# A squared-ReLU layer as seven block products: the second layer of blocks 1 to 8 with fewer multiplications and more sums

## The chip, the cores and the metric

The kernel runs on one NeuronCore of a Trainium2 chip. A core has a matrix engine (TensorE, in the profile PE, with its weight loads shown as PEld), three engines for elementwise work (VectorE or DVE, ScalarE or ACT, GpSimd or POOL) and a queue engine (SyncE or SP) that issues most transfers. Each engine works through its own instructions in order and waits for others by semaphores. PE writes into PSUM, eight banks of 128 partitions x 512 fp32 values; DVE and ACT read PSUM, POOL does not. The metric is the time of one execution in microseconds of device time. Before the change its median is 312.25 us in three runs (311.99 to 312.39).

## The reference

Attention over a sliding window of 64 positions (8 batches, 8 heads, 576 positions, head size 64), and on its output a feed-forward layer with a squared ReLU. All inputs and the output are fp32.

```python
scores = scale * np.matmul(q, k.transpose(0, 1, 3, 2))
mask = (rel >= 0) & (rel < window)          # window = 64
attn = softmax(np.where(mask, scores, -1e9))
x = np.matmul(attn, v).transpose(0, 2, 1, 3).reshape(4608, 512)
h = np.maximum(x @ w_in, 0.0)               # w_in  512 x 2048
out = (h * h) @ w_out                       # w_out 2048 x 512
```

## The kernel before

The 4608 tokens are nine blocks of 512: blocks 0 to 7 are the first 512 positions of each batch, and block 8 collects the last 64 of all batches. A block has four attention units (pairs of heads, `hp`), then layer 1 and layer 2. Everything that PE multiplies is fp16, and it sums in fp32.

Small functions each do one step of one unit or block, and the kernel calls them in an order written out by hand, which is each engine's order of work:

- `T` transposes q and k of a unit on PE (blocks 1 and 2; later blocks are transposed by DMA), and ACT or DVE copies them out of PSUM (`qk`).
- `Sc` multiplies q and k into `at_ps[i]`, two tiles of two banks, and ACT takes the exponential (`pm`, L281). `M` applies the mask as a minimum (DVE, L288). `AV` multiplies with v, again into `at_ps[i]`, and `N` divides (DVE, L311 and L314, `xs`); `A` is both. `X` transposes `xs` on PE into the bank of `ps_tr` and ACT or DVE copies it into `xT`.
- `F1(g, f)` is chunk f of layer 1: four matmuls of 512 columns into one of the two `ps_f1` banks (L337); DVE takes the positive part (`hr`, L340), ACT squares it into `h2` (L341). A block has 16 chunks.
- `F2(g, ts, quarter, ...)` is a quarter of layer 2 for 128 tokens: four matmuls of 512 columns (L372). After the fourth quarter ACT scales the bank into `osb` (L376) and SP stores it. A block has 16 such calls. `F2_last` does the last 128 tokens in two halves of 256 columns (L388), to store the first earlier.

Block 0 runs alone at first. Then F2 of block 0 runs beside the attention of block 1, F1 of block 1 beside that of block 2, written out call by call. From there a loop over n = 1 to 8 takes F2 of block n and F1 of block n + 1 together. The string `order` says which comes when ("2" an F2 call, "1" an F1 call); the list `fill` made from it has 32 entries, called slots here. `put(i, ...)` hangs other work in front of slot i: Sc, M, A and X of block n + 2, two units at a time. So Sc of two units stands at slot 8, M at 11 and 12, A of both at 14, X at 18 and 20, and the other two units ten slots later.

Inputs arrive as fp32 in staging tiles of 128 x 512 (`piece`, 24 of them), are cast to fp16 (mostly by POOL) and, for q and k of blocks 3 to 8, transposed by a DMA. `next_part` issues one load, its cast, and the transpose of the piece four before; a rule in the loop sets how many are issued by each slot. Loads, transposes and stores all stand in SP's queue, in program order. A tile pool gives a buffer again only when everything that reads it is done.

Of the kernel before, what the change touches and what calls it, by code (L numbers as in the profile page):

```python
# [8 lines left out]
FP32 = mybir.dt.float32  # L9
# [6 lines left out]
def kernel(  # L16
# [23 lines left out]
    X_SCALE = 16.0  # L40
# [4 lines left out]
    stp = ctx.enter_context(tc.tile_pool(name="stp", bufs=24))  # L45
    p16p = ctx.enter_context(tc.tile_pool(name="p16p", bufs=8))
# [270 lines left out]
    def X(g, hp, engine=nc.scalar, pool=ps_tr, tag="tr"):  # L317
# [3 lines left out]
        tr = pool.tile([P, 2, 512], FP16, name="xtr", tag=tag)  # L321
# [46 lines left out]
    def F2(g, ts, quarter, pool, tag):  # L368
# [5 lines left out]
        if quarter == 3:  # L374
            osb = opool.tile([P, DM], FP32, name="osb", tag="osb", bufs=5)
            nc.scalar.activation(out=osb[:], in_=f2[g, ts][:], func=AF.Copy, scale=OUT_SCALE)  # L376
            to_store.append((g, ts, osb))
        if quarter == 1 or g == seq[-1]:
            while to_store:
                store(*to_store.pop(0))  # L380

    def F2_last(g, ts):

        for half, (pool, tag) in enumerate(((ps_f2, "f2"), (ps_f1, "f1"))):
            cols = slice(half * 256, half * 256 + 256)
            t = pool.tile([P, 512], FP32, name="ops", tag=tag)
            for f in range(FFC):
                nc.tensor.matmul(t[:, 0:256], h2[g][:, f, ts * P:(ts + 1) * P], w_out_sb[:, f, cols],  # L388
                                 start=(f == 0), stop=(f == FFC - 1))
            osb = opool.tile([P, DM], FP32, name="osb", tag="osb", bufs=5)  # L390
            nc.scalar.activation(out=osb[:, 0:256], in_=t[:, 0:256], func=AF.Copy, scale=OUT_SCALE)  # L391
            for par, queue in enumerate((nc.sync, nc.scalar)):
                r = (2 * ts + par) * S + 512
                queue.dma_start(out=out[r:r + 64, cols], in_=osb[par * 64:(par + 1) * 64, 0:256])
# [5 lines left out]
    with tc.manual_schedule():  # L400
# [84 lines left out]
        for hp in range(2):  # L485
            cast_qk_pair(g1, "q", hp, nc.gpsimd)
            cast_qk_pair(g1, "k", hp, nc.gpsimd)
# [69 lines left out]
        F(8, second); T(g1, 2, engine=nc.vector); F(1, second)  # L557
# [13 lines left out]
        for _ in range(8):  # L571
            next_part()
        F(3, first)
# [91 lines left out]
```

## Time and profile before

| | before |
|---|---|
| time, median of three runs | 312.25 us |
| span of the profiled execution | 309.2 us |
| PE, DVE, ACT, POOL busy | 299.9, 162.7, 171.6, 117.5 us |
| layer 1 matmuls of 512 columns (L337) | 560, busy 137.6 us |
| layer 2 matmuls of 512 columns (L372) | 560, busy 136.1 us |
| layer 2 matmuls of 256 columns (L388) | 32, busy 3.7 us |
| hr (L340), squares (L341), osb (L376): mean of one | 689, 630, 587 ns |
| granted TensorE clock | 1.000 |

The profile is of one execution. The busy time of an engine counts overlapping instructions once; matmuls are pipelined, so the mean duration of one (379 ns for 512 columns) is longer than the distance from one to the next, and costs are read from distances. The span leaves out what lies before the first and after the last instruction; the profiled execution's own whole time is not given apart from its span, so the median stands beside it. The profile's chain of waits goes back from the last instruction to what released each one, and the engine that holds most of it sets the time.

### The profile page before, as it was taken

What the parts mean: (1) busy time and instruction counts of PE and PEld (TensorE: products, weight loads), DVE (VectorE), ACT (ScalarE), POOL (GpSimd) and SP (SyncE); (2) the same over time, 40 slices, a digit from 0 to 9 for tenths busy, and PEclk for the clock granted to TensorE, in tenths of its full rate; (3) what the DMA queues carried; (4) which work ended last, traced back from release to release, by engine and by line L of the source; (5) the groups of instructions that cost most, each with busy time, mean ns of one, the idle gap of its engine ahead of it and who ended that gap; (6) DMA issues with size and microseconds to landing.
All of it is one profiled execution on the core that took longest, in us unless ns stands there. A gap on an engine that the chain in (4) does not pass through costs nothing.

```text
span 309.2 us, 6624 instructions
## 1 busy us (share of the span) xinstructions
PE 299.9 (97%) x2604; PEld 150.8 (49%) x2604; DVE 162.7 (53%) x278; ACT 171.6 (55%) x268; POOL 117.5 (38%) x212
## 2 busy tenths in 40 slices
PE   7899999999999999999999999999999999999995
PEld 5444445454445544544454444544554555444444
DVE  4676628587266727553755365537553655344300
ACT  4757736686367545753575367546744674444411
POOL 4578749963462382254365246322320000000000
PEclk9999999999999999999999999999999999999999
DMA  7999999999999998999998999999921001100023
GB/s 231 241 354 375 384 289 280 310 188 175 235 182 225 178 224 187 204 194 202 197 232 187 211 187 184 205 220 173 217 58 70 34 2 36 68 34 34 36 63 74
DMA packets 141759, 55.49 MB, mean 179 GB/s; under 512 B 125728, under 2 KB 134176, under 8 KB 141728
## 3 DMA queue, kind: packets, MB, share of 16 engines
q1 hardware_dynamic: 141568, 54.94, 82.8%
q8 instruction: 20, 0.33, 0.5%
q10 hardware_dynamic: 160, 0.13, 0.2%
q14 instruction: 11, 0.09, 0.1%
HBM read 38.80 MB, written 9.44 MB: 156 GB/s over the span
## 4 chain that ended last, share of the span: by engine, by line
PE 81%; ACT 0%; DVE 0%; issue 0%
PE hps L337 36%; PE ops L372 35%; PE at L304 3%; PE at L274 3%; PE xtr L323 2%; PE ops L388 1%; PE tr L243 0%; PE hps L353 0%; PE at L337 0%; ACT osb L376 0%; DVE xT L113 0%; ACT osb L391 0%
## 5 line engine op out<-in xcount | busy, mean ns | idle before, releaser
L340 DVE TENSOR_SCALAR hr<-hps 128x512 f32<-128x512 f32 x143 | 97.9, 689 | 107.6 <-PE hps L337 106.4
L341 ACT ACTIVATE h<-hr 128x512 f16<-128x512 f32 x144 | 90.3, 630 | 86.8 <-DVE hr L340 86.6
L337 PE MATMUL hps<-xT,w_in_sb 128*128 128x512 f16 x560 | 137.6, 379 | 0.2
L372 PE MATMUL ops<-w_out_sb,h 128*128 128x512 f16 x560 | 136.1, 379 | 0.3 <-ACT osb L376 0.3
L372 PEld LDWEIGHTS <-h 128*128 128x128 f16 x560 | 53.1, 98 | 61.5 <-issue 0.3
L337 PEld LDWEIGHTS <-w_in_sb 128*128 128x128 f16 x564 | 53.1, 98 | 59.2 <-issue 1.4
L113 POOL CAST v_ev<-st_v 128x512 f16<-128x512 f32 x34 | 23.5, 692 | 43.9 <-DMA st_v<-in_v_dram 43.9
L113 POOL CAST k<-st_k 128x512 f16<-128x512 f32 x36 | 23.1, 641 | 44.7 <-DMA st_k<-in_k_dram 44.4
L281 ACT ACTIVATE pm<-at 128x1024 f16<-128x1024 f32 x35 | 34.1, 1015 | 2.7 <-PE at L274 2.7
L376 ACT ACTIVATE osb<-ops 128x512 f32<-128x512 f32 x35 | 20.5, 587 | 25.2 <-PE ops L372 25.2
L314 DVE TENSOR_TENSOR xs<-at,rden 128x512 f16<-128x512 f32 x36 | 24.9, 691 | 1.2
L288 DVE TENSOR_TENSOR pm<-pm,mask 128x1024 f16<-128x1024 f16 x32 | 24.1, 768 | 2.5 <-ACT pm L281 2.5
L111 ACT ACTIVATE xT<-xtr 128x512 f16<-128x512 f16 x31 | 18.4, 593 | 8.1 <-PE xtr L323 8.1
L113 POOL CAST q<-st_q 128x512 f16<-128x512 f32 x31 | 18.3, 609 | 10.9 <-DMA st_q<-in_q_dram 8.8
L222 POOL CAST v_od<-st_v 64x512 f16<-64x512 f32 x30 | 19.0, 635 | 1.6
L304 PEld LDWEIGHTS <-pm 128*64 128x64 f16 x576 | 11.4, 110 | 8.8 <-issue 4.3
L323 PEld LDWEIGHTS <-xs 128*128 128x128 f16 x144 | 10.7, 98 | 7.5
L304 PE MATMUL at<-v_ev,pm 128*64 128x65 f16 x384 | 14.3, 198 | 0.0
L323 PE MATMUL xtr<-ident,xs 128*128 128x128 f16 x144 | 13.8, 219 | 0.0
L113 POOL CAST v_od<-st_v 64x384 f16<-64x384 f32 x23 | 12.3, 536 | 1.8 <-DMA st_v<-in_v_dram 0.7
L304 PE MATMUL at<-v_od,pm 128*64 128x65 f16 x192 | 10.4, 194 | 0.4 <-DVE v_od L113 0.3
L111 ACT ACTIVATE qk<-tr 128x1024 f16<-128x1024 f16 x7 | 7.1, 1013 | 5.5 <-PE tr L243 3.1
(55 smaller groups left out, 120.4 us busy)
## 6 DMA issues: line engine op xcount, KB each, us to landing
st_k<-in_k_dram SPq DMA_DIRECT2D x40, 256.0 KB, 3.9
st_q<-in_q_dram SPq DMA_DIRECT2D x32, 256.0 KB, 5.1
out_dram<-osb SPq DMA_DIRECT2D x32, 256.0 KB, 2.8
st_v<-in_v_dram SPq DMA_DIRECT2D x28, 256.0 KB, 3.8
st_w<-in_moe_w_out_dram SPq DMA_DIRECT2D x16, 256.0 KB, 5.4
st_v<-in_v_dram SPq DMA_DIRECT2D x24, 128.0 KB, 4.9
w_st<-in_moe_w_in_dram SPq DMA_DIRECT2D x4, 512.0 KB, 6.1
st_w<-in_moe_w_in_dram SPq DMA_DIRECT2D x8, 256.0 KB, 7.6
```

The source lines that it names most:

```text
L111: engine.activation(out=out, in_=in_, func=AF.Copy, scale=1.0)
L113: engine.tensor_copy(out=out, in_=in_)
L281: nc.scalar.activation(out=p[:, hh, :] if apart else p[:], in_=sc[hh] if apart else both[:], func=AF.Exp, scale=1.0 / float(D) ** 0.5)
L288: nc.vector.tensor_tensor(out=p[:], in0=p[:], in1=m.unsqueeze(1).broadcast_to([P, 2, 512]), op=ALU.min)
L304: nc.tensor.matmul(a[jj * 64:(jj + 1) * 64, hh, jp * VW:jp * VW + D + 1], pm[g, hp][:, hh, j * 64:(j + 1) * 64], vsel, start=True, stop=True)
L314: nc.vector.tensor_tensor(out=x[:].rearrange("p j h d -> p h j d"), in0=a[:, :, :, 0:D], in1=rden[:].unsqueeze(3).broadcast_to([P, 2, 4, D ...
L323: nc.tensor.transpose(out=tr[:, 0, jp * P:(jp + 1) * P], in_=xs[g, hp][:, jp, :, :], identity=ident[:])
L337: nc.tensor.matmul(hps[:], w_in_sb[:, c, f * P:(f + 1) * P], xT[g][:, c, :], start=(c == 0), stop=(c == DMC - 1))
L340: nc.vector.tensor_scalar(out=hr[:], in0=hps[:], scalar1=0.0, scalar2=None, op0=ALU.max)
L341: nc.scalar.activation(out=h2[g][:, f, :], in_=hr[:], func=AF.Square)
L372: nc.tensor.matmul(f2[g, ts][:], h2[g][:, f, ts * P:(ts + 1) * P], w_out_sb[:, f, :], start=(f == 0), stop=(f == FFC - 1))
L376: nc.scalar.activation(out=osb[:], in_=f2[g, ts][:], func=AF.Copy, scale=OUT_SCALE)
```

## The change

Layer 2 of a block multiplies A (512 tokens x 2048) with B (2048 x 512). The change cuts both into 2 x 2 blocks (256 tokens, 1024 of the inner dimension, 256 columns) and computes the four blocks of the result with seven products in place of eight, after Strassen and Winograd. Four sums of blocks of B (`T_sum`, once for the whole kernel, each 128 partitions x 2048 fp16) and four sums of blocks of A (`S_sum`, for each block and each half s of 128 tokens, each 128 x 1024 fp16) are made by DVE. A product is eight matmuls of 256 columns for 128 tokens. A block has seven products for each of two halves s, in the order 1, 2, 6, 5, 7, 3, 4 (`L2S`).

Products 1, 6, 7 and 4 add up in half s of the bank `chain`; 2, 5 and 3 use the two halves of the bank `side`. After each product the bank's present sum is scaled into `osb` by ACT (products 1, 6, 5, 4) or added to what `osb` holds by DVE (2, 7, 3). Stores are issued at product 6 of each half, for the tiles finished by then. `chain` keeps the one `ps_f2` bank and `side` the one `ps_tr` bank for the rest of the kernel, so X goes into the first bank of its unit's own `at_ps` tile. `F2_last` is gone; block 0 still uses F2.

`fill` has 30 entries ("2" is now a product), and 14 in the last block. The S sums of half 0 of block n + 1 stand at slots 17 (27 in block 1) and 28, those left at slots 3 to 7 of its own layer 2. X comes at slots 16 and 17, and 27 and 28. T sum 1 stands in F2 of block 0, two calls before T of block 1's unit 2; T sums 2, 3 and 4 stand in F1 of block 1, before its chunk 0, before its chunk 7 and after its chunk 10, S3 of block 1 right behind the last of them, and S1, S2 and S4 behind chunk 15.

The sums need 32 KB per partition. The staging tiles go from 24 to 10, and the space of the sums serves as 16 more for the first 60 pieces; four casts of block 1 are called earlier for that, in the same place of POOL's order. The fp16 buffers of q and k go from 8 to 6 each. The scale of x goes from 16 to 8.

```diff
--- before.py
+++ after.py
-    X_SCALE = 16.0
+    X_SCALE = 8.0
...
-    stp = ctx.enter_context(tc.tile_pool(name="stp", bufs=24))
-    p16p = ctx.enter_context(tc.tile_pool(name="p16p", bufs=8))
+    stp = ctx.enter_context(tc.tile_pool(name="stp", bufs=10))
+    p16p = ctx.enter_context(tc.tile_pool(name="p16p", bufs=6))
...
+    wsum = const.tile([P, 8, 512], FP32, name="wsum")
+    hsum = const.tile([P, 8, 512], FP32, name="hsum")
+    T_sb = wsum[:].bitcast(FP16).rearrange("p a b -> p (a b)").rearrange("p (k c d) -> p k c d", k=4, c=8)
+    S_sb = hsum[:].bitcast(FP16).rearrange("p a b -> p (a b)").rearrange("p (k c d) -> p k c d", k=4, c=8)
+    staged = [0]
     def piece(*key):
-        st[key] = stp.tile([P, 512], FP32, name="st_" + "".join(str(x)[0] for x in key[:1]), tag="st")
+        k = staged[0] % 26
+        staged[0] += 1
+        if staged[0] > 60 or k < 10:
+            st[key] = stp.tile([P, 512], FP32, name="st_" + "".join(str(x)[0] for x in key[:1]), tag="st")
+        elif k < 18:
+            st[key] = wsum[:, k - 10, :]
+        else:
+            st[key] = hsum[:, k - 18, :]
...
-    def X(g, hp, engine=nc.scalar, pool=ps_tr, tag="tr"):
+    def X(g, hp, engine=nc.scalar, pool=ps_tr, tag="tr", own=None):
         if g not in xT:
             xT[g] = xtpool.tile([P, DMC, 512], FP16, name="xT", tag="xT")
-        tr = pool.tile([P, 2, 512], FP16, name="xtr", tag=tag)
+        if own is not None:
+            tr = at_ps[own][:, 0, :].bitcast(FP16).rearrange("p (a b) -> p a b", a=2)
+        else:
+            tr = pool.tile([P, 2, 512], FP16, name="xtr", tag=tag)
...
-            to_store.append((g, ts, osb))
-        if quarter == 1 or g == seq[-1]:
+            to_store.append(lambda: store(g, ts, osb))
+        if quarter == 1:
             while to_store:
-                store(*to_store.pop(0))
-    def F2_last(g, ts):
...
+                to_store.pop(0)()
...
+    HF = FFC // 2
+    HC = DM // 2
+    osbs = {}
+    def b_of(i, j):
+        return w_out_sb[:, i * HF:(i + 1) * HF, j * HC:(j + 1) * HC]
+    def a_of(g, i, j, s):
+        t0 = 256 * i + 128 * s
+        return h2[g][:, j * HF:(j + 1) * HF, t0:t0 + 128]
+    def t_of(k):
+        return T_sb[:, k - 1]
+    def s_of(k, s):
+        return S_sb[:, k - 1, :, 128 * s:128 * s + 128]
+    def minus(out, a, b, op=ALU.subtract, engine=None):
+        (engine or nc.vector).tensor_tensor(out=out, in0=a, in1=b, op=op)
+    def T_sum(k):
+        if k == 1:
+            minus(t_of(1), b_of(0, 1), b_of(0, 0))
+        elif k == 2:
+            minus(t_of(2), b_of(1, 1), t_of(1))
+        elif k == 3:
+            minus(t_of(3), b_of(1, 1), b_of(0, 1))
+        else:
+            minus(t_of(4), b_of(1, 0), t_of(2))
+    def S_sum(g, k, s):
+        if k == 1:
+            minus(s_of(1, s), a_of(g, 1, 0, s), a_of(g, 1, 1, s), ALU.add)
+        elif k == 2:
+            minus(s_of(2, s), s_of(1, s), a_of(g, 0, 0, s))
+        elif k == 3:
+            minus(s_of(3, s), a_of(g, 0, 0, s), a_of(g, 1, 0, s))
+        else:
+            minus(s_of(4, s), a_of(g, 0, 1, s), s_of(2, s))
+    def product(to, a, b, start):
+        for f in range(HF):
+            nc.tensor.matmul(to, a[:, f, :], b[:, f, :], start=start and f == 0, stop=f == HF - 1,
+                             skip_group_check=True)
+    def flush():
+        while to_store:
+            to_store.pop(0)()
+    def L2S(g, p, s, banks):
+        chain, side = banks
+        c, pa, pb = chain, side[:, 0:HC], side[:, HC:2 * HC]
+        lo, hi = slice(0, HC), slice(HC, 2 * HC)
+        def scaled(out, in_):
+            nc.scalar.activation(out=out, in_=in_, func=AF.Copy, scale=OUT_SCALE)
+        def plus(o, in_):
+            nc.vector.scalar_tensor_tensor(out=o, in0=in_, scalar=OUT_SCALE, in1=o, op0=ALU.mult, op1=ALU.add)
+        if p == 1:
+            for i in range(2):
+                osbs[s, i] = opool.tile([P, DM], FP32, name="osb", tag="osb", bufs=5)
+        up, dn = osbs[s, 0], osbs[s, 1]
+        if p == 1:
+            product(c, a_of(g, 0, 0, s), b_of(0, 0), True)
+            scaled(up[:, lo], c)
+        elif p == 2:
+            product(pa, a_of(g, 0, 1, s), b_of(1, 0), True)
+            plus(up[:, lo], pa)
+        elif p == 6:
+            product(c, s_of(2, s), t_of(2), False)
+            scaled(up[:, hi], c)
+            flush()
+        elif p == 5:
+            product(pb, s_of(1, s), t_of(1), True)
+            scaled(dn[:, hi], pb)
+        elif p == 7:
+            product(c, s_of(3, s), t_of(3), False)
+            plus(dn[:, hi], c)
+        elif p == 3:
+            product(pb, s_of(4, s), b_of(1, 1), False)
+            plus(up[:, hi], pb)
+            to_store.append(lambda: store(g, s, up))
+            if g == seq[-1]:
+                flush()
+        else:
+            product(c, a_of(g, 1, 1, s), t_of(4), False)
+            scaled(dn[:, lo], c)
+            if g == seq[-1] and s == 1:
+                for par, queue in enumerate((nc.sync, nc.scalar)):
+                    r = (2 * (2 + s) + par) * S + 512
+                    queue.dma_start(out=out[r:r + 64, lo], in_=dn[par * 64:(par + 1) * 64, lo])
+            else:
+                to_store.append(lambda: store(g, 2 + s, dn))
+                if g == seq[-1]:
+                    flush()
+        if g == seq[-1] and s == 1 and p == 7:
+            for par in range(2):
+                r = (2 * (2 + s) + par) * S + 512
+                nc.sync.dma_start(out=out[r:r + 64, hi], in_=dn[par * 64:(par + 1) * 64, hi])
+    ORDER = (1, 2, 6, 5, 7, 3, 4)
...
+        for hp in range(2):
+            cast_qk_pair(g1, "q", hp, nc.gpsimd)
+            cast_qk_pair(g1, "k", hp, nc.gpsimd)
...
-        F(8, second); T(g1, 2, engine=nc.vector); F(1, second)
+        F(6, second); T_sum(1); F(2, second); T(g1, 2, engine=nc.vector); F(1, second)
...
+        T_sum(2)
         F(3, first)
         Sc(g2, 0); F(1, first); T(g2, 1); F(1, first); M(g2, 0); F(2, first)
+        T_sum(3)
         Sc(g2, 1); A(g2, 0); F(1, first); T(g2, 2); F(1, first); M(g2, 1); F(2, first)
-        X(g2, 0, nc.vector)
+        X(g2, 0, nc.vector); T_sum(4)
         for _ in range(4):
             next_part()
-        Sc(g2, 2); A(g2, 1); F(1, first); T(g2, 3); F(1, first); M(g2, 2); F(2, first)
-        X(g2, 1, nc.vector); F(1, first)
+        S_sum(g1, 3, 0)
+        Sc(g2, 2); A(g2, 1); F(1, first); T(g2, 3); F(1, first); M(g2, 2); F(3, first)
+        X(g2, 1, nc.vector)
+        for k in (1, 2, 4):
+            S_sum(g1, k, 0)
...
+        chain = ps_f2.tile([P, 512], FP32, name="chain", tag="f2")
+        side = ps_tr.tile([P, 512], FP32, name="side", tag="tr")
         for n in range(1, NBLK):
             g = seq[n]
             one = seq[n + 1] if n < NBLK - 1 else None
+            second = iter([lambda p=p, s=s: L2S(g, p, s, (chain[:, s * HC:(s + 1) * HC], side))
+                           for s in range(2) for p in ORDER])
             if one is not None:
-                first = [lambda f=f: F1(one, f) for f in range(FFC)]
-                second = [lambda ts=ts, i=i: F2(g, ts, i, ps_f2, "f2") for ts in range(4) for i in range(4)]
-                a, b = iter(first), iter(second)
-                order = ("2222" + "11" + 2 * "212121211" + "21221211" if n > 1 else
-                         "22222222" + 2 * "11211211212" + "11")
-                fill = [next(a if c == "1" else b) for c in order]
+                a = iter([lambda f=f: F1(one, f) for f in range(FFC)])
+                order = ("22222222" + "11211121112111211" + "11122" if n == 1 else
+                         ("222121121211211" if n == 2 else "221212112121211") + "212121121121122")
             else:
-                fill = [lambda ts=ts, i=i: F2(g, ts, i, *((ps_f2, "f2") if ts % 3 == 0 else (ps_f1, "f1")))
-                        for ts in range(3) for i in range(4)] + [lambda: F2_last(g, 3)]
+                order = "2" * 14
+            fill = [next(a if c == "1" else second) for c in order]
             at = {}
             def put(i, *work):
@@ -605,28 +718,35 @@
             if n == 1:
                 put(0, lambda: Sc(g2, 3), lambda: A(g2, 2))
                 put(2, lambda: M(g2, 3))
-                put(3, lambda: X(g2, 2))
-                put(4, lambda: A(g2, 3))
-                put(6, lambda: X(g2, 3))
-            for work in later:
-                put(1, work)
+                put(3, lambda: X(g2, 2, own=1))
+                put(5, lambda: A(g2, 3))
+                put(7, lambda: X(g2, 3, own=1))
+            for i, work in enumerate(later):
+                put(1 + i, work)
             later = []
+            for i, (k, s) in zip((3, 4, 5, 6, 7) if n > 1 else (1, 1, 2, 4, 6),
+                                 ((4, 0), (1, 1), (2, 1), (3, 1), (4, 1))):
+                if n > 1 or (k, s) != (4, 0):
+                    put(i, lambda k=k, s=s: S_sum(g, k, s))
+            if one is not None:
+                put(27 if n == 1 else 17, lambda: S_sum(one, 3, 0))
+                put(28, lambda: S_sum(one, 1, 0), lambda: S_sum(one, 2, 0))
             base = 4 * (n + 2)
-            for i, x, two in ((12 if n == 1 else 8, (9, 11) if n == 1 else (10, 12), units[base:base + 2]),
-                              (21 if n == 1 else 18, (9, None) if n == 1 else (10, 12), units[base + 2:base + 4])):
+            for i, x, two in ((12 if n == 1 else 8, (8, 9), units[base:base + 2]),
+                              (22 if n == 1 else 19, (None, None) if n == 1 else (8, 9), units[base + 2:base + 4])):
                 for t, u in enumerate(two):
                     if u is not None:
                         put(i, lambda u=u, t=t: Sc(*u, i=t))
                         put(i + 3 + t, lambda u=u: M(*u))
                         put(i + 6, lambda u=u, t=t: A(*u, i=t))
                         if x[t] is None:
-                            later.append(lambda u=u: X(*u))
+                            later.append(lambda u=u, t=t: X(*u, own=t))
                         else:
-                            put(i + x[t], lambda u=u: X(*u))
+                            put(i + x[t], lambda u=u, t=t: X(*u, own=t))
             for i, group in enumerate(fill):
                 for work in at.pop(i, []):
                     work()
-                total = 12 + (32 * (n - 1) + i + 1) * (len(load_list) - 12) // 150
+                total = 12 + (30 * (n - 1) + i + 1) * (len(load_list) - 12) // 140
```

More of the change, by code (lines that the diff above doesn't have):

```diff
@@ L376, in F2 @@
             nc.scalar.activation(out=osb[:], in_=f2[g, ts][:], func=AF.Copy, scale=OUT_SCALE)
-            to_store.append((g, ts, osb))
-        if quarter == 1 or g == seq[-1]:
+            to_store.append(lambda: store(g, ts, osb))
+        if quarter == 1:
             while to_store:
-                store(*to_store.pop(0))
-    def F2_last(g, ts):
[L384 to L394, printed above, removed]
+                to_store.pop(0)()
```

3 lines of the change are left out of this document (removed).

## The prediction

> **What bounds the kernel now.** I read the busy shares and the chain of waits first, then the groups of instructions, then stretches of the timeline. The first three lines are the page's busy shares and the chain that ended last.
>
> ```profile
> PE 299.9 (97%) x2604; PEld 150.8 (49%) x2604; DVE 162.7 (53%) x278; ACT 171.6 (55%) x268; POOL 117.5 (38%) x212
> ...
> PE 81%; ACT 0%; DVE 0%; issue 0%
> PE hps L337 36%; PE ops L372 35%; PE at L304 3%; PE at L274 3%; PE xtr L323 2%; PE ops L388 1%; PE tr L243 0%; PE hps L353 0%; PE at L337 0%; ACT osb L376 0%; DVE xT L113 0%; ACT osb L391 0%
> ```
>
> PE is the bound, and half of it is layer 2. Next, DVE has 47% of the span free, but not evenly. Stretches of the span, with each engine's busy time: the first layer of block 1, then one whole later block.
>
> ```profile
> 56.47:74.46 17.99, 17.93 (x203) 9.48 (x203) 14.67 (x26) 15.18 (x22) 11.69 (x20) 1.00 1.08 230
> 173.41:204.75 31.34, 31.34 (x273) 15.38 (x272) 16.49 (x28) 17.68 (x28) 13.66 (x23) 1.00 1.11 199
> ```
>
> The columns are length, PE, PEld, DVE, ACT and POOL. In the early stretch DVE is free for only 3.3 us. In a later block PE is never idle and DVE is free for 14.9 us. Third, what a 256-column matmul costs, and how long a bank stays shut. The timeline at the kernel's end, then around 78 us (us of start, us of length):
>
> ```profile
> 301.61 3.59 PEld L388 LDWEIGHTS <-h 128*128 128x128 f16 x32
> 301.82 3.66 PE L388 MATMUL ops<-w_out_sb,h 128*128 128x256 f16 x32
> ...
> 303.82 0.38 ACT L391 ACTIVATE osb<-ops 128x256 f32<-128x256 f32 x1 [1.15 <-PE ops L388]
> ```
>
> ```profile
> 77.13 1.03 PE L372 MATMUL ops<-w_out_sb,h 128*128 128x512 f16 x4
> ...
> 78.20 0.60 ACT L376 ACTIVATE osb<-ops 128x512 f32<-128x512 f32 x1 [0.27 <-PE ops L372]
> ...
> 78.84 1.89 PE L372 MATMUL ops<-w_out_sb,h 128*128 128x512 f16 x8 [0.31 <-ACT osb L376]
> ```
>
> 32 loads and matmuls run in (305.2-301.8)/31 = 110 ns each (first and last start), so the 98 ns load hides behind the matmul. A 512-column one takes 216 ns (four in 0.864 us, the later blocks' step). PE finishes feeding the bank at 77.13+0.86 = 77.99; the eviction starts 0.2 later, and PE enters the same bank again only at 78.84. Last, two DVE stretches: what PE waits for at 46 us, and what the mask's minimum costs.
>
> ```profile
> 44.67 1.23 DVE L113 COPY qk<-tr 128x1024 f16<-128x1024 f16 x1 [0.46 <-PE tr L243]
> ```
>
> ```profile
> 45.95 0.41 PE L274 MATMUL at<-qk 64*128 64x64 f16 x16 [0.46 <-DVE qk L113]
> ```
>
> ```profile
> L288 DVE TENSOR_TENSOR pm<-pm,mask x32: 676/682/1101, 36.6 to 254.6; 128x1024 f16<-128x1024 f16 x32
> ```
>
> The minimum is the trace's only fp16 operation of two tensors in SBUF: 0.68 us per 1024 elements, up to 1.10.
>
> **The change part by part.**
>
> *Fewer columns.* Layer 2 of a block was 64 matmuls of 512: 64 x 0.216 = 13.82 us. It becomes 7 products x 2 halves x 8 = 112 matmuls of 256: 112 x 0.110 = 12.29 us. That is 1.54 less in seven blocks; the last one had 48 x 0.216 + 32 x 0.110 = 13.88 and saves 1.59. **-12.3 us**, all of it on PE.
>
> *DVE's new work per block.* Eight S sums of 1024 fp16 elements at 0.68 to 0.77 (median and mean of the minimum): 5.4 to 6.2. Six additions into osb: 256 fp32 columns, bounded by rden's 0.20 (8 columns) and xs' 0.69 (512 columns) and taken between them by columns, 0.44: 2.6. 16.5 becomes 24.5 to 25.3 of some 31 us. ACT loses four evictions of 0.58 and gains eight of 0.38: +0.7, no matter. So DVE fits in the mean; what counts is where its queue is late.
>
> *Neighbours on one bank.* The order 1,2,6,5,7,3,4 alternates between the chain and side banks, but 4 and the next 1 are both on chain. From the last column fed, the eviction starts 0.25 later (303.82 against 301.82+16x0.11 = 303.57), runs 0.38, and PE enters some 0.04 after: 0.67. Within the sequence a product of 0.88 lies between and hides it, if ACT or DVE comes at once. At the ends of blocks 1 to 7 nothing lies between (fill ends "22", and begins "2"), nor in the last block's middle. In blocks 2 to 6 ACT must first finish the copy of the X at slot 28, which leaves it some 0.15 late. 5 x 0.82 + 3 x 0.67 + 0.4 (block 1, an X between) = **+6.5**. The ends are 0, if only the same columns shut a bank (1 writes the other half), and 8 x 0.85 + 0.4 = 7.2 by the 512-column row. I take the wait: chain is one tile in one bank, and the nearest row is a bank waited for as a whole. The Trainium skill ("PSUM — Partial Sum Buffer", PSUM bank collisions raise a hardware error) says to guard PSUM by bank and quadrant, not by address. By that rule this term stays; guarded by address it would be 0. No run so far shows which.
>
> *X in its own bank.* ps_tr goes to side for good. X writes the bank that its unit's AV and N have left, so only the next Sc into it waits, for X's copy on ACT. At slot 19 that is near: hr, square, copy, copy stand behind two N (0.2+0.69 each), so X's second copy ends about 0.25 after PE gets there. Blocks 2 to 6: **+1.3** (0 to 2.5). Slot 8 follows X by nine slots, free.
>
> *T sum 1* (2048 elements, twice the minimum less one start: 1.25 us; 0.68 to 2.2) stands in front of the qk copy at 44.67, whose end PE already waits for. DVE comes free from the q cast at 44.22, so the copy starts at 45.4 to 45.9: **+1.0** (0 to 1.8).
>
> *T sums 2 to 4 and S3* fall into 56.47:74.46: 3 x 1.25 + 0.68 = 4.4 us against 3.3 free, so 1.1 at least if every gap is filled. They aren't: T sum 4, S3 and an N stand before the hr of chunk 11, and F1 of chunk 13 needs that bank (two f1 banks). Walking the queue, chunk 9 waits 0.6 and chunk 13 1.3, of which 0.3 is X moved behind: **+1.8** (1.1 to 4).
>
> *Block 1's head.* S1, S2 and S4 wait for the last square (1.6 after the last F1), so the N of g2's unit 2 ends 4.3 after it, not 1.9. Behind it: product 6 waits for ACT's Exp and eviction (0.3), X for N (0.6), product 5 for the addition of 2 (0.7). In all 2.0 with the bank wait counted above; the 0.3 of 78.84 goes away: **+1.5** (0.6 to 3).
>
> *Block ends.* At slot 28, S1 waits for the square of the last F1 (hr 0.27 + 0.69, square 0.63), then S2, then the addition of product 3, which product 2 of the next block needs for side. With 0.68 sums it is ready 0.1 to 0.2 before PE. POOL shares: two sums 0.1 each slower (mean minus median) use that up, and in blocks 1 to 5 the slow ones (1.1) go beyond it: **+1.0** (0 to 4). The Trainium skill ("SBUF — State Buffer", Who interferes with whom) says that a DVE instruction with two SBUF inputs contends with a GpSimd instruction that reads SBUF. The minimum's spread, 676 to 1101 ns, agrees; if every sum in blocks 1 to 5 met one, this would be nearer to 4.
>
> *DMA and queues.* 24 staging tiles become 10 (26 with the sums' space, for the first 60 pieces). SP issues each q or k transpose four pieces behind its load and waits there for POOL's cast, so a load never has more than some eight pieces open: 0 here; with that cover gone a load's 4 to 5 us would show at Sc. POOL's order is unchanged (the moved casts stand in the same place). p16p at 6 lets g3's third and fourth q and k wait for T of g2, over before their casts at 65 and 67: 0. Stores move to two points per block, for osb long done; SP loses waits. Scale 8 for 16: 0.
>
> *Tail.* Product 7's and 3's stores put four issues of 0.5 on SP ahead of the last one: **+0.5** (0 to 1).
>
> The sum: -12.3+6.5+1.3+1.0+1.8+1.5+1.0+0.5 = +1.3. The profiled execution's span is 309.2, so 310.5; some 3.05 lie outside it (to the median 312.25 of the three runs), which I keep: **313.5 us**. Some 0.2% (0.6 us) is what a measurement tells from no change.
>
> **The rivals.**
>
> A, faster: DVE's queue keeps up, in the first layer of block 1 above all. For it: F1 has two banks, and 47% of DVE is free. Against it: 4.4 us into 3.3. It decides there: if the last F1 ends no later than in the trace of before, the terms 1.3, 1.8 and 1.0 go, and 0.9 of block 1's head: 313.5-5.0 = 308.5.
>
> B, faster still: the chain bank's halves don't wait for each other. 313.5-6.5 = 307.0. Against it: one tile, one bank.
>
> C, slower: DVE becomes the bound, because the sums run at 1.1 us (the minimum's slowest). Per block 8 x 0.42 = 3.4 more, 28.5 of 31 with its waits on squares: PE late by about 1 us in five or six blocks (5.5), T sums 4 x 0.9 = 3.6, block 1's head 2: 324.6; halfway, at 0.9, it is 319. For it: POOL is busy 38% of the time; against it: 0.77 in the mean.
>
> **How the numbers follow.** Forecast 0.49 (311 to 316), A 0.26, B 0.05, C 0.20. The range 307.5 to 319.5 leaves out B, A's lower edge and C's upper half, some 0.18. Faster: A, B and 0.03 of the forecast, 0.34; same: 0.14 of the forecast (311.6 to 312.9); slower: its other 0.32 and C, 0.52.
>
> **What would show it.** 896 matmuls of 256 columns at 110 ns; PE idle about 0.7 to 0.8 at each block's start behind the eviction of product 4; the first F1 stretch some 1.8 longer, F1 waiting for hr; S sums at 0.7 to 0.8; blocks 3 to 6 at some 30.9 us against 31.35. It is wrong if the block ends show no wait (B), if the F1 stretch keeps its length (A), or if the sums take 1.1 (C).

## The result, and the profile after

| | before | after |
|---|---|---|
| time, median of five runs each, side by side | 311.99 us (311.63 to 312.39) | 314.59 us (313.15 to 314.81) |
| span of the profiled execution | 309.2 us | 313.1 us |
| PE, DVE, ACT, POOL busy | 299.9, 162.7, 171.6, 117.5 us | 290.8, 225.1, 173.2, 124.7 us |

The changed kernel is slower by 2.6 us: the ratio is 1.0072, with a 95% interval of 1.0051 to 1.0093, which leaves out 1. The forecast was 313.5 us. The profiled execution of the changed kernel took 314.78 us, 1.7 more than its span.

The page of the changed kernel, first its busy shares, then its chain of waits.

```profile
PE 290.8 (93%) x2972; PEld 185.6 (59%) x2972; DVE 225.1 (72%) x394; ACT 173.2 (55%) x299; POOL 124.7 (40%) x212
...
PE 4%; ACT 0%; issue 0%
PE chain L440 2%; PE side L440 2%; ACT osb L454 0%
```

PE works 9.1 us less and the span is 3.9 us longer, so PE now stands still some 13 us more. The chain says little here: it covers the last block only, where it breaks off. Before, it followed layers 1 and 2 through the whole kernel. So I read what PE waits for, with the columns engine, line, what it waited for, the sum in us, how often and the longest; then the groups of the S sums and the additions.

```profile
PE chain L440 <- ACT osb L454: 4.1, 9, 0.6
PE hps L353 <- DVE hr L356: 2.8, 3, 1.9
PE at L287 <- DVE qk L126: 2.3, 3, 1.5
PE side L440 <- DVE osb L457: 2.0, 5, 0.8
PE at L339 <- DVE xs L327: 1.5, 2, 0.8
```

```profile
L416 DVE TENSOR_TENSOR hsum<-h 128x1024 f16<-128x1024 f16 x32 | 23.3, 729 | 5.7 <-ACT h L357 5.7
L457 DVE SCALAR_TENSOR_TENSOR osb<-side,osb 128x256 f32<-128x256 f32 x32 | 13.4, 420 | 11.6 <-ACT osb L454 8.7 <-PE side L440 1.7 <-issue 1.2
```

Five waits hold 12.7 us, and each has its place. The nine on `chain` are the ends of blocks 1 to 7 and the two half blocks where products 4 and 1 meet. Two of the three on `hr` (0.73 and 1.85) are in the first layer of block 1. The longest on `qk` is T sum 1's. `side` and `xs` are in the head of block 1 and at the starts of the later blocks. Prices came out as costed: a product takes 0.874 us from start to start (109 ns a matmul), an S sum 0.73 (0.72 and 0.76 for the other kinds), an addition 0.42.

The stages of both kernels as stretches (length; busy time of PE, PEld, DVE, ACT, POOL; granted clock; DMA share; GB/s). The changed kernel's first layer of block 1 and blocks 2 and 4 (each from its first product to the next block's):

```profile
58.21:77.93 19.72, 17.12 (x170) 8.78 (x170) 18.35 (x28) 14.56 (x22) 14.57 (x22) 1.00 0.99 218
113.28:145.97 32.69, 30.70 (x329) 20.36 (x329) 25.73 (x47) 18.80 (x34) 18.75 (x30) 1.00 1.13 193
176.80:207.58 30.78, 30.08 (x321) 20.00 (x320) 23.70 (x43) 17.72 (x32) 13.04 (x22) 1.00 1.13 191
```

In the first line DVE is free for only 1.4 of 19.7 us; before, the stretch between the same marks (56.52 to 73.60) took 17.08 us with DVE busy for 13.99. In a whole block the kernel gains: 30.8 against 31.35 us. Over all stages, in us (the terms of the prediction put on the stage in which each falls):

| stage | before | after | difference | predicted |
|---|---|---|---|---|
| start, up to F2 of block 0 | 34.52 | 35.14 | +0.6 | 0 |
| F2 of block 0, up to Sc of unit 2 (T sum 1) | 11.43 | 12.50 | +1.1 | +1.0 |
| first layer of block 1 (T sums 2 to 4, S3) | 17.08 | 19.72 | +2.6 | +1.8 |
| block 1: Sc of block 2's last unit to block 2's first product | 33.44 | 35.35 | +1.9 | +1.0 |
| block 2 | 31.57 | 32.69 | +1.1 | -0.3 |
| blocks 3 to 6 | 125.39 | 122.76 | -2.6 | -1.0 |
| block 7 | 27.62 | 26.72 | -0.9 | -0.9 |
| block 8, up to the end of its matmuls | 13.69 | 13.06 | -0.6 | -0.9 |
| tail | 3.9 | 4.6 | +0.7 | +0.5 |

The 10.57 us between the second and the third stage are the same in both. The differences add up to that of the spans: 3.9 measured, 1.3 predicted (1.2 by the rounded rows). The kernel gains 4.1 us from block 3 on up to the tail and loses 7.3 before. The spans are of one execution each, and some of the 3.9 is their choice: the medians lie only 2.6 apart.

Four places in the changed kernel's timeline (start and length in us, engine, line, operation; in brackets the idle time before it and what ended it). T sum 1, ahead of the copy that PE waits for:

```profile
45.23 1.22 DVE L416 TENSOR_TENSOR wsum<-w_out_sb 128x2048 f16<-128x2048 f16 x1
46.37 1.22 DVE L126 COPY qk<-tr 128x1024 f16<-128x1024 f16 x1
47.64 0.41 PE L287 MATMUL at<-qk 64*128 64x64 f16 x16 [1.50 <-DVE qk L126]
```

PE's wait was 0.46 and is 1.50. The first layer of block 1, T sums 3 and 4 and S3, and the chunk behind them:

```profile
64.94 1.56 DVE L416 TENSOR_TENSOR wsum<-w_out_sb 128x2048 f16<-128x2048 f16 x1
...
70.93 1.51 DVE L416 TENSOR_TENSOR wsum<-w_out_sb,wsum 128x2048 f16<-128x2048 f16 x1
72.36 1.09 DVE L416 TENSOR_TENSOR hsum<-h 128x1024 f16<-128x1024 f16 x1
...
74.21 1.28 DVE L356 TENSOR_SCALAR hr<-hps 128x512 f32<-128x512 f32 x2
74.95 2.83 PE L353 MATMUL hps<-xT,w_in_sb 128*128 128x512 f16 x12 [1.85 <-DVE hr L356]
```

DVE works without a break from 70.59, and the hr that PE needs stands behind 3.3 us of sums and N. The sums are slow here: 1.56, 1.51 and 1.09 us, where T sum 1 took 1.22 and an S sum takes 0.73 in the mean. The slow ones have company: in this trace the 36 S sums during which POOL does nothing take 0.69 at most, and each of the 11 that take 0.82 or more overlaps an instruction of POOL, as do these three. Overlap does not always slow a sum (15 others that overlap took 0.69 or less), and POOL's times in a profile are rough. Then the end of a late block, 4 into 5, with S1 and S2 between a square and an addition:

```profile
206.07 1.04 PE L440 MATMUL chain<-wsum,h 128*128 128x256 f16 x8
206.69 0.69 DVE L416 TENSOR_TENSOR hsum<-h 128x1024 f16<-128x1024 f16 x1 [0.75 <-ACT h L357]
207.14 0.38 ACT L454 ACTIVATE osb<-chain 128x256 f32<-128x256 f32 x1
207.41 0.98 DVE L416 TENSOR_TENSOR hsum<-hsum,h 128x1024 f16<-128x1024 f16 x1
207.58 1.03 PE L440 MATMUL chain<-w_out_sb,h 128*128 128x256 f16 x8 [0.47 <-ACT osb L454]
208.32 0.41 DVE L457 SCALAR_TENSOR_TENSOR osb<-side,osb 128x256 f32<-128x256 f32 x1
208.78 1.03 PE L440 MATMUL side<-w_out_sb,h 128*128 128x256 f16 x8 [0.17 <-DVE osb L457]
```

Product 4 is fed to the end at 206.07 + 8 x 0.109 = 206.94; product 1 starts 0.64 later, behind the eviction. Product 2 then waits 0.17 for the addition of product 3, which stood behind both sums. The start of block 2 has both waits and a third:

```profile
113.28 1.03 PE L440 MATMUL chain<-w_out_sb,h 128*128 128x256 f16 x8 [0.47 <-ACT osb L454]
114.96 0.40 PE L339 MATMUL at<-ident,xs 128*128 128x128 f16 x4 [0.64 <-DVE xs L327]
116.12 1.03 PE L440 MATMUL side<-w_out_sb,h 128*128 128x256 f16 x8 [0.77 <-DVE osb L457]
```

S1 and S2 (112.35 to 114.06) stand here ahead of two N as well, which X waits for, and the addition stands last (115.66).

### The profile page after: what moved, and what is told of

It is laid out like the page before. It is cut to its first block, busy times and chain, and to the rows that moved or that the text cites. A ratio compares the mean times of both kernels' runs of the same rounds, so it can differ in the third digit from the quotient of the medians.

```text
span 313.1 us, 7538 instructions
## 1 busy us (share of the span) xinstructions
PE 290.8 (93%) x2972; PEld 185.6 (59%) x2972; DVE 225.1 (72%) x394; ACT 173.2 (55%) x299; POOL 124.7 (40%) x212
## 5 line engine op out<-in xcount | busy, mean ns | idle before, releaser
L440 PEld LDWEIGHTS <-hsum 128*128 128x128 f16 x512 | 48.3, 98 | 13.4 <-issue 0.7
L440 PEld LDWEIGHTS <-h 128*128 128x128 f16 x384 | 37.2, 98 | 15.2 <-issue 8.0
L440 PE MATMUL chain<-wsum,hsum 128*128 128x256 f16 x256 | 33.3, 273 | 0.2 <-DVE hsum L416 0.2
L454 ACT ACTIVATE osb<-chain 128x256 f32<-128x256 f32 x48 | 18.1, 378 | 22.5 <-PE chain L440 21.3
L416 DVE TENSOR_TENSOR hsum<-h 128x1024 f16<-128x1024 f16 x32 | 23.3, 729 | 5.7 <-ACT h L357 5.7
L440 PE MATMUL chain<-w_out_sb,h 128*128 128x256 f16 x128 | 16.6, 272 | 4.1 <-ACT osb L454 4.1
L440 PE MATMUL side<-w_out_sb,h 128*128 128x256 f16 x128 | 16.6, 272 | 1.5 <-DVE osb L457 1.4
L440 PE MATMUL side<-wsum,hsum 128*128 128x256 f16 x128 | 16.6, 273 | 0.5 <-DVE osb L457 0.5
L124 ACT ACTIVATE xT<-at 128x512 f16<-128x512 f16 x26 | 15.2, 585 | 2.9 <-PE at L339 2.9
L440 PE MATMUL side<-w_out_sb,hsum 128*128 128x256 f16 x128 | 16.6, 273 | 0.0
```

Source lines behind the costliest of these rows:

```text
L124: engine.activation(out=out, in_=in_, func=AF.Copy, scale=1.0)
L416: (engine or nc.vector).tensor_tensor(out=out, in0=a, in1=b, op=op)
L440: nc.tensor.matmul(to, a[:, f, :], b[:, f, :], start=start and f == 0, stop=f == HF - 1, skip_group_check=True)
L454: nc.scalar.activation(out=out, in_=in_, func=AF.Copy, scale=OUT_SCALE)
```

## The experiments

The theory after the result: PE's saving is there in full, and goes into three things: products 4 and 1 on one bank at the block ends; S1 and S2 in DVE's queue ahead of the addition of product 3 (and ahead of N in block 1); and the T sums and block 1's own sums in the start. The rival: DVE as a whole is near its limit, so that taking one wait away brings up the next. All runs stood beside runs of the kernel before (312.1, 312.0 and 311.9 us in three series).

**S1 and S2 one slot later.** The products' order is untouched; the two sums stand behind the addition of product 3 in DVE's queue.

```diff
-                put(28, lambda: S_sum(one, 1, 0), lambda: S_sum(one, 2, 0))
+                put(29, lambda: S_sum(one, 1, 0), lambda: S_sum(one, 2, 0))
```

> Only the place of S1 and S2 of half 0 changes: behind product 3 at the block's end (slot 29) instead of ahead of it (slot 28), so that the addition of product 3 and, in block 1, two N no longer stand behind a sum that waits for the last square. Theory (in-order DVE queue, not DVE's load): block 2 loses its 0.64 us wait for xs and 0.77 us wait for side, blocks 3 to 5 their 0.28, 0.23 and 0.17: 2.1 us less, 312.5 us, with the waits for the chain bank unchanged. Rival (DVE is simply full): the same work in another order gains nothing, 314.6 us.

Measured: 310.24 us (309.37 to 311.23), ratio to before 0.9948 (0.9926 to 0.997): with this one slot's difference the kernel is no longer slower than before but 1.9 us faster, 2.3 below what was expected. Blocks 2 and 4 as stretches:

```profile
110.86:141.83 30.97, 30.37 (x329) 20.43 (x328) 26.04 (x46) 18.70 (x34) 18.28 (x28) 1.00 1.03 199
172.40:202.79 30.39, 29.92 (x321) 19.99 (x320) 23.96 (x43) 17.71 (x32) 13.90 (x22) 1.00 1.06 190
```

Block 2 falls from 32.69 to 30.97, blocks 3 to 6 from 122.76 to 121.74 in all, so 2.7 us are shown to be the queue's order. The medians lie 4.35 apart, so 1.6 are not shown to come from it. The two profiled executions lie further apart still (314.78 and 309.37), and most of the rest stands ahead of the edit, where both kernels have the same instructions: in this one F2 of block 0 begins 1.45 us earlier, and PE's wait behind T sum 1 is 0.58, not 1.50. Why the medians should share such a difference stays open.

**The other bank first in half 1.** Half 1 swaps `chain` and `side`, so that product 4 of half 1 and product 1 of the next block lie on different banks.

```diff
-            second = iter([lambda p=p, s=s: L2S(g, p, s, (chain[:, s * HC:(s + 1) * HC], side))
+            second = iter([lambda p=p, s=s: L2S(g, p, s, ((chain[:, 0:HC], side), (side[:, 0:HC], chain))[s])
```

> Only the roles of the two banks change: half 0 keeps its sum in one bank and its side products in the other, half 1 the other way round, so that product 4 and the next product 1 lie in different banks. Theory: the 0.64 us behind ACT goes, but product 1 now needs the addition of product 3, which stands on DVE behind S1 and S2 and ends some 1.2 us after product 4; so 0.9 us more at six block ends and 1.1 at block 2, 0.9 less inside blocks 1 and 8: about 320 us, slower than the changed kernel. Rival (the neighbours' wait is all there is): nine waits less, about 308.6 us.

Measured: 320.96 us (317.5 to 321.22), ratio 1.0255 (1.0203 to 1.0307), which is slower as expected. Product 3 is now on `chain`, and with it the addition that stands behind S1 and S2; product 1 itself waits for it. The waits, the start of block 2, and that stretch's granted clock (the third column from the right):

```profile
PE chain L440 <- DVE osb L457: 13.2, 7, 3.6
```

```profile
110.42 0.98 DVE L416 TENSOR_TENSOR hsum<-hsum,h 128x1024 f16<-128x1024 f16 x1
...
113.00 0.41 DVE L457 SCALAR_TENSOR_TENSOR osb<-chain,osb 128x256 f32<-128x256 f32 x1
113.47 1.87 PE L440 MATMUL chain<-w_out_sb,h 128*128 128x256 f16 x8 [3.58 <-DVE osb L457]
```

```profile
113.47:117.69 4.22, 4.22 (x25) 3.22 (x25) 0.13 (x1) 0.98 (x2) 2.67 (x5) 0.50 0.87 219
117.69:121.00 3.31, 3.31 (x23) 2.35 (x22) 2.04 (x4) 0.98 (x2) 0.62 (x1) 0.80 1.07 131
```

The same edit that removes one wait (0.64 a block) brings 1.4 to 3.6 a block from the queue behind it. In the profiled execution PE's clock also fell behind the longest; the last section comes back to it.

**Both.** The two edits together.

> Both of the edits before: roles of the banks swapped for half 1, and S1 and S2 behind product 3. Theory: the addition of product 3 ends before product 4 does, so nothing shuts the bank of the next product 1: 2.1 us of the sums' place and 8 x 0.66 us of neighbour waits go, 307.2 us, and no wait for ACT's or DVE's eviction is left at the block ends. Rival (the waits only turn into others, since PE was not the bound there): no more than the 2.1 us, 312.5 us.

Measured: 306.35 us (305.98 to 306.94), ratio 0.982 (0.9794 to 0.9847). Block 4:

```profile
172.87:202.63 29.76, 29.76 (x323) 20.02 (x320) 24.62 (x43) 17.77 (x33) 13.45 (x22) 1.00 1.11 199
```

PE is not idle for a moment in blocks 3 to 6. 31.35 - 29.76 = 1.59 us is what the smaller number of columns is worth in a block, undisturbed; the prediction had 1.54. Against the run with the sums behind, 30.39 - 29.76 = 0.63 is the bank. So both causes are shown, and neither edit would have shown the other's size alone: the swap of banks gains 3.9 us (310.24 to 306.35) with the sums behind, and loses 6.4 (314.59 to 320.96) without, in part by the clock.

**Staging, casts and scale alone, and X in its unit's bank alone.** Two kernels without the products, on the old F2. The first has all of the change's buffers, casts and scale and keeps X in `ps_tr`; the second puts X, from block 2's last two units on, into its unit's own bank too, at the old slots.

```diff
-    stp = ctx.enter_context(tc.tile_pool(name="stp", bufs=24))
-    p16p = ctx.enter_context(tc.tile_pool(name="p16p", bufs=8))
+    stp = ctx.enter_context(tc.tile_pool(name="stp", bufs=10))
+    p16p = ctx.enter_context(tc.tile_pool(name="p16p", bufs=6))
...
-                            put(i + x[t], lambda u=u: X(*u))
+                            put(i + x[t], lambda u=u, t=t: X(*u, own=t))
```

(The last pair of lines is in the second kernel only.)

> The kernel before with 10 staging tiles and the 16 places of the sums' space, fp16 q and k buffers 6, the four casts called earlier, scale 8; x is transposed in the bank of its own pool as before. Theory: the 7 us that the kernel without products lost came from X in the attention banks at the old places (X at slots 18 and 20 around the Sc at slot 18, which waited for ACT's copies), not from the staging: 312.0 us within 0.6. Rival (fewer staging tiles slow the start or the loads): 314 us or more.

> The kernel before with everything of the change but the products and sums: staging tiles 10 (and the 16 places of the sums' space for the first 60 pieces), fp16 q and k buffers 6, four casts called earlier, x transposed in its unit's own bank, scale 8. Theory: nothing of it lies on PE's path, 312.0 us within 0.6. Rival (the fewer staging tiles delay loads, or X in the attention bank delays Sc): 0.25 us for each of ten X pairs or more, 313 to 316 us.

Measured: 311.06 us (310.29 to 312.22) for the first, ratio 0.9972 (0.9957 to 0.9986), and 319.36 (318.24 to 320.12) for the second, ratio 1.0237 (1.0211 to 1.0262). The first shows the price of the staging, the fewer fp16 buffers, the moved casts and the scale: nothing, if anything a gain of 0.9, a little more than the 0.6 allowed for. The second was expected at 312.0 and missed by 7 us. Its largest wait, and the longest of its six places:

```profile
PE at L285 <- ACT xT L122: 6.7, 6, 1.8
```

```profile
98.80 0.64 PE L285 MATMUL at<-qT,kT 64*128 64x64 f16 x32 [1.78 <-ACT xT L122]
```

With X at slots 18 and 20 and the next Sc at 18, X's copies have not left the bank when Sc comes. The changed kernel has X at 16 and 17 and Sc at 19, and shows this wait once (0.57 at 104.14, in block 1, where X stands at 20 and 21 and Sc at 22). So the moved slots go with putting X there; the expectation had overlooked them.

**Short S sums.** On the kernel with both edits, the S sums of blocks 2 to 8 are cut to one eighth of their elements. The rest of the sums is left out, so part of the layer's computation is missing; the time tells what DVE's load costs.

```diff
+    def cut(g, out, a, b, op=ALU.subtract):
+        if g == seq[1]:
+            minus(out, a, b, op)
+        else:
+            minus(out[:, 0:1], a[:, 0:1], b[:, 0:1], op)
```

> The kernel with the banks' roles changed and the sums behind product 3 (306.35 us), in which the S sums of blocks 2 to 8 take an eighth of the elements (128 of 1024; the rest of each sum is left as block 1 made it, so that part of the computation is left out). It takes some 4 us of DVE's work out of each of those blocks. Theory (DVE's work hides; only its order costs): 306.35 us within 0.6. Rival (DVE's load of 75% delays PE everywhere, or sums contend with POOL): 0.5 us or more in each of seven blocks, 302.8 us or less.

Measured: 305.28 us (305.15 to 306.34), ratio 0.9797 (0.9773 to 0.982); the interval overlaps with that of the full sums. The median is 1.1 us lower, more than the 0.6 allowed for and far from the 3.5 of the rival. Block 4 again:

```profile
171.59:201.35 29.76, 29.76 (x322) 20.00 (x320) 20.50 (x43) 17.75 (x33) 12.10 (x21) 1.00 1.05 191
```

DVE does 4.1 us less in the block, and the block is no shorter: 29.76 both times. Once the queue's order is right, the S sums of the later blocks lie beside PE's work. The rival theory, DVE as the bound, falls for them.

**The T sums earlier.** On the kernel with both edits, T sums 1 and 2 go ahead of the third and fourth q cast of block 1, T sum 3 behind X of its unit 2, and only T sum 4 stays ahead of its first layer.

```diff
-        for hp in range(2, HP):
-            cast_qk_pair(g1, "q", hp, nc.vector)
-        F(6, second); T_sum(1); F(2, second); T(g1, 2, engine=nc.vector); F(1, second)
+        T_sum(1)
+        cast_qk_pair(g1, "q", 2, nc.vector)
+        T_sum(2)
+        cast_qk_pair(g1, "q", 3, nc.vector)
+        F(8, second); T(g1, 2, engine=nc.vector); F(1, second)
...
-        X(g1, 1, nc.scalar, *in_f1); X(g1, 2, nc.vector)
+        X(g1, 1, nc.scalar, *in_f1); X(g1, 2, nc.vector); T_sum(3)
...
-        T_sum(2)
+        T_sum(4)
         F(3, first)
...
-        T_sum(3)
...
-        X(g2, 0, nc.vector); T_sum(4)
+        X(g2, 0, nc.vector)
```

> The kernel with the banks' roles changed and the sums behind product 3 (306.35 us), and the four T sums moved to where DVE is idle: T1 ahead of block 1's third q cast, T2 ahead of the fourth, T3 behind the copy of X(block 1, unit 2), T4 alone ahead of chunk 0 of F1. Theory (4.4 us of sums into 3.3 us of free DVE time make F1 of block 1 wait): the stretch from F1's third chunk of block 1 to the first product shrinks from 20.1 to some 17.9 us, 304.1 us in all. Rival (F1's waits there come from something else, such as S3 or the staging): no change, 306.3 us.

Measured: 304.09 us (303.46 to 304.24), ratio 0.9751 (0.973 to 0.9772). The first layer of block 1, in this kernel and then in the one before it with both edits:

```profile
57.08:74.03 16.95, 16.78 (x173) 8.65 (x173) 14.92 (x26) 14.84 (x22) 11.44 (x19) 1.00 1.05 219
```

```profile
57.43:77.25 19.82, 17.23 (x170) 8.80 (x171) 18.36 (x28) 14.98 (x22) 13.77 (x22) 1.00 0.98 211
```

The stretches have slightly other ends, so I compare from the third chunk of the first layer to the first product: 17.61 against 20.08 us, 2.5 less, with 17.36 in the kernel before the change. So the loss in this stage is shown to come from the T sums that stood in it; of the three, T sum 4 still does. A second series with this kernel gave 303.83 us (303.42 to 305.08), expected at 304.1:

> The kernel of t_sums_moved once more, beside head_reordered on one chip: 304.1 again, within 0.6. If it comes out 0.6 or more away, differences of that size between runs of two calls say nothing.

**Block 1's own sums later.** On top of that: S1, S2 and S4 of block 1 behind the N of block 2's third unit, the sums of its half 1 at slots 9, 10, 15 and 20 (the head); and the last two A of block 1 at slot 29 with S1 and S2 behind them (the end). First both parts, then the head alone.

```diff
-                put(0, lambda: Sc(g2, 3), lambda: A(g2, 2))
+                put(0, lambda: Sc(g2, 3), lambda: A(g2, 2), lambda: S_sum(g1, 1, 0), lambda: S_sum(g1, 2, 0))
+                put(2, lambda: S_sum(g1, 4, 0))
...
-            for i, (k, s) in zip((3, 4, 5, 6, 7) if n > 1 else (1, 1, 2, 4, 6),
+            for i, (k, s) in zip((3, 4, 5, 6, 7) if n > 1 else (1, 9, 10, 15, 20),
...
-                        put(i + 6, lambda u=u, t=t: A(*u, i=t))
+                        put(29 if n == 1 and i == 22 else i + 6, lambda u=u, t=t: A(*u, i=t))
```

(The last pair is the end, left out in the kernel with the head alone.)

> As the one before, and DVE's order at the start of the loop changed: S1, S2 and S4 of block 1 behind the N of block 2's unit 2 instead of ahead of it, the sums of block 1's half 1 spread over slots 9 to 20 instead of 1 to 6, and at the end of block 1 the last two A behind product 3. Theory (the 2.2 us that block 1's head lost are DVE's order): 1.5 us less there and 0.4 less at block 2's first product, 302.2 us. Rival (the head is bound by ACT and the banks): 304 us, as without it.

> t_sums_moved with only the first half of start_reordered: the sums 1, 2 and 4 of block 1's half 0 stand behind the N of block 2's third unit, those of half 1 at slots 9, 10, 15 and 20; A of the last two units and the sums at slot 28 and 29 stay where t_sums_moved has them. Theory: block 1, from its first product to block 2's, keeps its length of about 24.5, its head loses the 1.7 that start_reordered showed for p1 to p1, less the 0.3 of the longer first stretch, and block 2 stays at 30.2 instead of 31.1: 304.1 - 1.7 + 0.3 = 302.7. Rival: start_reordered's gain in block 1 came from A at slot 29, and the head alone gives nothing: 304.1.

Measured: 303.94 us (303.06 to 304.5) with both, ratio 0.9747 (0.9725 to 0.977), and 303.46 (302.81 to 304.67) with the head alone, ratio 0.9723 (0.9693 to 0.9752). Neither can be told from 304.09 and 303.83; both expectations of a gain missed. From block 1's first product to block 2's it takes 34.68 and 34.90 us without these edits, 34.58 with the head alone and 33.01 with both; block 2 takes 30.20 without, 30.26 with the head alone and 31.10 with both. The head's kernel, where product 6 of block 1 starts:

```profile
77.80 1.05 PE L440 MATMUL chain<-wsum,hsum 128*128 128x256 f16 x8 [0.86 <-DVE hsum L416]
```

X no longer waits for N (0.81) nor product 5 for an addition (0.53); instead product 6 waits 0.86 for S2 itself, at 77.80. So the head's waits are traded, as the rival had it, and the 1.67 in block 1 (34.68 to 33.01) came from the end. Of that 0.90 is given back in block 2, where product 6 waits 0.72 for S2, now behind two N; the rest does not show in the medians.

The best version is the one with both edits and the T sums moved: 304 us, 2.5% faster than before.

## Why the prediction was right

The sign, the time (314.59 in 307.5 to 319.5) and the mechanism as a whole are right: PE saves what was worked out and loses more than that at the blocks' seams and in DVE's queue. The sign was no safe call (0.52 for slower), and that the sum came so near is partly luck, because the terms erred both ways. The banks and X were put 2.3 us too high together; the first layer of block 1, block 1 and block 2 came out 3.1 above what was put there.

- *Fewer columns, -12.3:* right. With no wait left, a block is 1.59 shorter (1.54 predicted), in the run with both edits.
- *Neighbours on one bank, +6.5:* the mechanism is right, and rival B falls. Measured from the last column fed: 0.64 at six ends and in the middle of the last block, 0.74 at block 2's end, 0.25 of idle in the middle of block 1: 5.5. The 0.15 for a late ACT showed at block 2's end alone; at block 4's the copy ended at 207.15, just as the eviction could start. Product 1 writes other columns than those being evicted, and waits all the same. The Trainium skill ("PSUM — Partial Sum Buffer", PSUM bank collisions raise a hardware error) says to guard PSUM by bank and not by address, and the kernel's waits do so; whether the chip would have borne the two side by side no run tried.
- *X in its own bank, +1.3:* the step failed. No Sc of blocks 2 to 6 waited; one of block 1 did, 0.57. The walk put X's second copy 0.25 behind PE's arrival, and it was there in time. The kernel with X at the old slots shows that the wait itself is real (6.7 us in six places).
- *T sum 1, +1.0:* 1.07 here; the copy started 1.05 after the q cast's end, as walked. But four other profiled executions have the same instructions up to there, and in them the stage is only 0.13, 0.01, 0.29 and 0.01 longer than before (the runs with the sums behind, the banks alone, both, and the short sums). The last q cast ahead of T sum 1 started 9.75 us after the first matmul of F2 here, and 8.81, 8.52, 8.96 and 8.54 there: the later that cast, the larger the term. So the 1.07 met the term by luck.
- *T sums 2 to 4 and S3, +1.8:* the mechanism and the two chunks are right (0.73 and 1.85 for the predicted 0.6 and 1.3), the size is too small. The step that failed is the duration: T sums at 1.25 and S3 at 0.68. T sums 3 and 4 and S3 took 1.56, 1.51 and 1.09 there, 1.0 more in all, with POOL busy for 14.57 of the 19.72 us. In the run with both edits T sum 4 took 1.22, and the second wait was 1.55, not 1.85. The Trainium skill ("SBUF — State Buffer", Who interferes with whom) says that such sums contend with POOL instructions that read SBUF. The overlaps above agree, but no run took POOL's work away.
- *Block 1's head, +1.5:* with the columns, the bank in the middle and the bank at the end, block 1 was put at +1.0 and came to +1.9. The three waits walked through are there: product 6 0.18 (0.3 predicted, but for ACT, and it was for S2), X for N 0.81 (0.6), product 5 for the addition 0.53 (0.7). What was missed lies later: Sc behind X's copy 0.57, and 0.18 for an hr.
- *Block ends, +1.0:* this is the step that failed most. Blocks 3 to 5 show the wait behind S1 and S2 at their starts, 0.28, 0.23 and 0.17, about as predicted, and block 6 none. But block 2's start was treated like theirs. At slot 28 of block 1 two A stand behind S1 and S2, so X and product 2 wait for the sums: 0.64 and 0.77. Block 2 is +1.1 for the predicted -0.3, and the one-slot edit made it 1.72 shorter.
- *DMA and queues, 0:* right, by the kernel with the staging alone. *Tail, +0.5:* 0.7.
- *What lies outside the span, 3.05:* it is 1.7 to 1.8 in all executions of the changed kernel whose time and span are both known. The 3.05 set one execution's span against the median of others; with 1.75, before's profiled execution would be 310.95, some 1.0 below its median, while the changed kernel's is 0.2 above its own. So some 1.2 of the 3.9 between the spans is the choice of executions, and 1.3 of the 3.05 carried the forecast from a short execution to the median. Against the medians the terms were short by 1.3: 1.3 forecast, 2.6 measured.

Rival A (DVE keeps up) falls in the first layer of block 1, rival C by the price of the S sums (0.73, not 1.1) and by the run with short sums. Blocks 3 to 6, at 30.4 to 30.8, are a little better than the 30.9 foreseen, since the Sc wait is absent. (The prediction's own terms, with 0.2 for a block's end, make 31.1 of blocks 3 to 5 and not 30.9.)

## What to carry to other kernels

An odd number of products that alternate between two banks ends on the bank where the next round begins: count it through to the seam, and swap the banks each round. In an in-order queue, put whatever frees a bank ahead of sums that wait for another engine; one slot was worth 2.7 us in these blocks, and the swap of banks, right in itself, cost 6.4 us until that was done. Work that is done once goes where its engine idles (here behind the casts' waits for data), not into the stage in which that engine has 3 us left.

## What the runs showed of the hardware

Behind a wait of 3.58 us PE ran at a lower clock: in the profiled execution of the kernel with only the banks swapped, the stretch behind that wait shows a granted clock of 0.50 for 4.2 us and 0.80 for the next 3.3, and a product took (115.13 - 113.47) = 1.66 us and not 0.87. That is 4.22 x 0.50 + 3.31 x 0.20 = 2.8 us beyond the wait itself; behind the other waits of that kernel on the same addition (1.4 to 1.95) the clock is 1.00. The loss does not come in every execution: the shortest one of that kernel (317.5 us) had a mean clock of 1.000. The Trainium skill ("TensorE: Matmul & The Clock Gate", Part 1: The HAM clock gate) states a fall to half the clock after an idle window of some 3.4 us, and the trace agrees.

The start of the kernel varies: F2 of block 0 began at 35.14, 33.69, 34.22 and 35.16 us in four profiled executions with the same instructions up to there. Differences of a microsecond between two profiles are therefore read from one mark to the next in the later stages, and not from the spans.
